# A long-convolution and expert-selection kernel: the filter layers in array quarters, earlier spectrum loads, and a shorter search round

## The chip, the cores and the metric

The kernel runs on one core of one Trainium2 chip. The metric is the device time of one execution, in microseconds (us). TensorE (PE) multiplies, VectorE (DVE) and ScalarE (ACT) can read the multiplier's result memory (PSUM), GpSimd (POOL) works on the on-chip buffer memory (SBUF) only, and SyncE (SP) issues nearly all transfers. Each engine takes its instructions in program order; between engines there are semaphores.

## The reference

```
h_mlp  = maximum(pos_emb @ w1, 0) @ w2          # 12608 x 64 -> 64 -> 128 channels
h_filt = h_mlp * exp(-0.01 * pos)[:, None]      # the decay
u = x * v                                       # 4 batches x 12608 x 128
y = irfft(rfft(u, 2S) * rfft(h_filt, 2S))[:S]   # causal convolution of every channel
a = x * y
scores = a @ w_gate                             # one number for each position
idx = the 128 positions of a batch with the largest scores
ye = maximum(a[idx] @ w1m, 0) @ w2m             # 128 -> 1024 -> 128
out = a;  out[idx] = a[idx] + sigmoid(scores[idx]) * ye
```

## The kernel before

The convolution's transform of length 25530 is split as 111 x 230, and every array lies as 111 x 115 positions. The program is written out in order by hand; the order of the code is the order on each engine.

1. **Filter layers** (`h_hid`). The positions come in 15 chunks of four columns of 111 positions in each of two halves h (the last chunk has two). Both halves share one input tile: half 0 on partitions 0 to 63, half 1 on 64 to 127. L282 multiplies a chunk by a block matrix with `w1` twice on its diagonal, 128 x 128, 444 columns; an ACT relu (L283) takes it to SBUF; then L291 multiplies by `w2`, eight matmuls of 64 rows, 128 columns. Before the second layer of chunk k-1 stands the first layer of chunk k. L300 and L304 (DVE) and L302 (POOL) multiply the result by the decay, with and without a sign pattern, and write it to `hb`: two DVE instructions for half 0, one for half 1, and from the latter one POOL instruction.
2. **Filter transform** (`h_spec`). For 32 groups of four channels: fold (L327, on DVE for groups 0 and 1, else on POOL), first transform (L336), ACT copy (L339), second transform (L356), then ACT L358 and four DVE instructions (L361 to L364), and the spectrum of the group goes to the DRAM tile `hd` (L365). The buffers of this result are the three named `ht`.
3. **Main loop**, 128 steps t (4 batches x 32 groups): transform the data (`f_s1`, L226/L227, and `dft`, L243), combine (L376, L377), multiply by the spectrum (`f_y`, L384 to L387; the spectrum is loaded from `hd` into `ht` by `load_h`, L221, two steps ahead), POOL L393/L394, back transform `f_i` (three steps later). `load_u` (L209) loads the data four steps ahead, `stage_u` (L215, L216, POOL) prepares them. Before the loop, L769 loads zeros (`zr`) into the padding rows of the `xa` buffers, which the next part uses.
4. **End of a batch** (`P1.run`), 29 steps h: last transform stage, L456 multiplies by x, L459 (DVE) by the gate weights, four ACT instructions (L473) sum each row into the scores; then L495 masks them.
5. **Search** (`TopK`, `TopKS`): 16 rounds find the 128th largest score bit pair by bit pair. A round counts scores over three candidates (L560), PE sums the counts over the partitions, L570 gives the step `up`, L577 (`move`) adds it to the next candidates. For batches 0 to 2 the rounds run on ACT in the background of the next batch (`TopKS`); for batch 3 they run alone on DVE at the end (`TopK`).
6. **Selection and experts** (`select`, `place`, `moe`): the positions are gathered (L711), transposed (L723), put through the two expert layers and scattered back. Batch 3's part has a run of 12 matmuls with no result that is used (L720, `NWARM`) ahead of the transposition.

Of the kernel before, what the change touches and what calls it, by code (L numbers as in the profile page):

```python
# [12 lines left out]
ALU = mybir.AluOpType  # L13
# [5 lines left out]
NQ = 64  # L19
# [24 lines left out]
NWARM = 12  # L44
# [91 lines left out]
def hyena_moe(ctx, tc, xg, x2, pos, bw, ww, wg, mw1, mw2, fo, c1, gx, cf, ci, wm, tk, zr, out):  # L136
# [112 lines left out]
    def h_hid():  # L249
        pt, hid = view(arena, POS0, [128, PJ, N1]), view(arena, HID0, [128, PJ, N1])  # L250
        wl = buf("u", NU - 1, [128, 2, 128])
        nc.gpsimd.memset(hb[:, :, :, N3:], 0.0)
        bwt, wwt = wl[:, 0], wl[:, 1]
        nc.sync.dma_start(bwt, bw)
        ch = [(a, min(a + PC, PJ)) for a in range(0, PJ, PC)]
# [22 lines left out]
        for k in range(len(ch) + 1):  # L278
            if k < len(ch):
                a, z = ch[k]  # L280
# [3 lines left out]
            if not k:  # L284
                continue
            a, z = ch[k - 1]
            ps = ps2(k % 2, [N1, 2, PC, D], f"hm_{k}")
            for i in range(z - a):
                for h in range(2):
                    if h * PJ + a + i < N3:  # L290
                        nc.tensor.matmul(ps[:, h, i], lhsT=hid[h * FO:(h + 1) * FO, a + i],  # L291
                                         rhs=wwt[h * FO:(h + 1) * FO], start=True, stop=True)
            for h in range(2):
                j0 = h * PJ + a
                j1 = min(h * PJ + z, N3)
                w = j1 - j0
                o = hb[:, :, :, j0:j1]
                pv = ps[:, h, :w].rearrange("p j d -> p d j")
                wb = wm_sb[:, :, j0:j1].unsqueeze(2).to_broadcast([N1, 3, D, w])
                nc.vector.tensor_tensor(out=o[:, 0], in0=pv, in1=wb[:, 0], op=ALU.mult)  # L300
                if h:
                    nc.gpsimd.tensor_tensor(out=o[:, 1], in0=o[:, 0], in1=wb[:, 1], op=ALU.mult)  # L302
                else:
                    nc.vector.tensor_tensor(out=o[:, 1], in0=pv, in1=wb[:, 2], op=ALU.mult)  # L304

    def h_spec():
# [39 lines left out]
        for g in range(NG):  # L346
# [13 lines left out]
            ht = buf("ht", g, [128, 2, HC])  # L360
# [5 lines left out]
            if g >= NG - 3:  # L366
                stage_u(g - NG + 3)

# [39 lines left out]
    class P1:  # L408
# [42 lines left out]
        def fin(self, h):  # L451
            ja, n = hbs[h]
            k = ja // 8
            xa = self.xa[k]
# [4 lines left out]
            nc.vector.tensor_tensor(out=wx, in0=xa[:, js], in1=self.wg.unsqueeze(1).to_broadcast([128, n, D]),  # L459
                                    op=ALU.mult)  # L460
            self.acc = wx, ja, n
            if ja + n == blocks[k][1]:
                j0, j1 = blocks[k]
                for t in range(2):
                    nc.sync.dma_start(out[self.b, t * PR:(t + 1) * PR, j0:j1], xa[t * NQ:t * NQ + PR, :j1 - j0])
                if k:
                    self.load_a(k - 1 + NX)
# [9 lines left out]
        def run(self, bg):  # L477
# [16 lines left out]
            self.reduce()  # L494
# [30 lines left out]
    class TopK:  # L525
# [32 lines left out]
        def counts(self, r):  # L558
            for i in range(3):
                nc.vector.tensor_scalar(out=self.ms[i % 2], in0=self.key, scalar1=self.cand[:, i + 1:i + 2], scalar2=0.0,  # L560
                                        op0=ALU.is_ge, op1=ALU.add, accum_out=self.cnt[:, i:i + 1])
            if r % 8 < 7:
                nc.vector.tensor_scalar(out=self.nx, in0=steps[:, r % 8 + 1], scalar1=self.cand[:, 0:1], scalar2=None,
                                        op0=ALU.add)
# [9 lines left out]
        def move(self, r):  # L574
            if r % 8 < 7:
                self.cand = self.cd[r % 2]
                nc.vector.tensor_scalar(out=self.cand, in0=self.nx, scalar1=self.up, scalar2=None, op0=ALU.add)  # L577
            else:
                nc.vector.tensor_tensor(out=self.top, in0=self.cand[:, 0:1], in1=self.up, op=ALU.add)
# [48 lines left out]

    def select(b, k, n, tr, ones, rs, ws):
# [17 lines left out]
        mm2(ps[:, 0:1], tr, cnt[:, 1:2], start=False, stop=True)  # L647
        lim = small([128, 1], f"lim_{b}", tag="lim")
# [17 lines left out]
        t = tots(sn[:, n - 1:n], tr, 1, f"bs_{b}", 3)[0][1]  # L666
        en = small([128, 1], f"en_{b}", tag="en")
# [37 lines left out]
    def moe(b, ix, ws, mb, ks):  # L705
# [11 lines left out]
        if b + 1 == B:  # L717
            wp = ps1(1, [128, 128], "warm")
            for _ in range(NWARM):
                nc.tensor.matmul(wp, lhsT=ident, rhs=ident, start=True, stop=True)  # L720
# [43 lines left out]
    for t in bank1 + bank2:  # L764
# [11 lines left out]
    for t in range(NT + LAG):  # L776
# [4 lines left out]
        if t < NT:  # L781
# [16 lines left out]
            load_h(t + 2)  # L798
# [24 lines left out]
def _layout(inputs):  # L823
# [14 lines left out]
    bw = np.zeros((2 * FO, 2 * FO), w1.dtype)  # L838
    bw[:FO, :FO] = w1
    bw[FO:, FO:] = w1  # L840
    named = [("xg", xg), ("x2", x2), ("pos", pg), ("bw", bw), ("ww", np.concatenate([w2, w2]))]
# [30 lines left out]
```

## Time and profile before

| | |
|---|---|
| three runs, median (lowest to highest) | 1013.59 us (1012.2 to 1017.33) |
| the profiled execution: its own time | 1017.58 us |
| its span, first to last instruction | 1015.6 us |
| TensorE's granted clock over the span | 0.97 of full |
| busy: PE, DVE, POOL, ACT | 932.6, 891.0, 745.7, 598.2 us |

Line numbers (L282) are those of the kernel before. In the rows below, a row of the timeline or of the chain begins with its start and its length in microseconds; xN is the number of instructions merged into it, and an fp32 matmul counts twice there; in brackets stands the idle time of the engine ahead of it, and what ended that. The granted clock is 1.00 at 2.4 GHz and 0.50 at 1.2 GHz.

### The profile page before, as it was taken

Reading aid. Unit: us, or ns where it says so; the run is one execution under the profiler, and the core shown is the slowest. Engines: PE = TensorE matmul, PEld = TensorE weight load, DVE = VectorE, ACT = ScalarE, POOL = GpSimd, SP = SyncE. Lnnn points to the kernel's source line nnn. Section 1 sums busy time; section 2 is a strip of 40 time slices with the busy share of each in tenths; the row PEclk is TensorE's granted clock in tenths of the full one; section 3 lists DMA queues with packets and bytes.
Section 4 is the critical chain, followed back from the end, with each engine's and each line's share of the span. In section 5 each row is a group of like instructions: output and inputs, shape, how many; then the busy total and the mean of one; then the engine's idle time right before and its main releaser. Section 6 shows DMA issues by size and latency. Waiting matters only on the chain.

```text
span 1015.6 us, 38023 instructions
## 1 busy us (share of the span) xinstructions
PE 932.6 (92%) x15620; PEld 823.2 (81%) x15620; DVE 891.0 (88%) x1563; ACT 598.2 (59%) x1961; POOL 745.7 (73%) x704
## 2 busy tenths in 40 slices
PE   8799979999999999999989999999999999989914
PEld 5577759988889898888889888888898888879804
DVE  7799969999998899999987999999878999986883
ACT  2255525555547887854478878544588786446710
POOL 4888838988887488988965689889765888754500
PEclk9899989999999999999999999999999999999956
DMA  8044486665776865657778656568686666544820
GB/s 240 2 168 177 183 220 179 194 181 176 217 217 222 282 179 173 196 167 199 222 234 266 194 179 196 171 183 242 198 280 197 190 181 183 162 150 140 292 69 6
DMA packets 64961, 190.58 MB, mean 188 GB/s; under 512 B 8725, under 2 KB 15876, under 8 KB 64772
## 3 DMA queue, kind: packets, MB, share of 16 engines
q1 hardware_dynamic: 64532, 187.63, 60.3%
q8 instruction: 123, 2.02, 0.9%
q0 software_dynamic: 256, 0.52, 0.2%
q14 instruction: 50, 0.41, 0.1%
HBM read 146.70 MB, written 41.42 MB: 185 GB/s over the span
## 4 chain that ended last, share of the span: by engine, by line
DVE 43%; PE 39%; DMA 10%; issue 4%; ACT 1%; SPq 1%; DVEq 1%; POOL 0%; POOLq 0%; ACTq 0%
DVE arena L384 8%; PE a L226 8%; DVE c L385 8%; PE a L243 7%; PE c L226 7%; DMA arena<-in_x_dram 6%; DVE c L377 5%; DVE c L376 5%; DVE arena L387 4%; DVE arena L386 4%; PE a L448 3%; DMA out_dram<-arena 3%; PE a L336 3%; PE c L336 3%; DVE arena L456 3%
## 5 line engine op out<-in xcount | busy, mean ns | idle before, releaser
L243 PE MATMUL a<-arena,cf_sb 128*64 128x222 f32 x2048 | 230.2, 356 | 19.1 <-DVE c L377 17.8
L226 PE MATMUL c<-ci_sb,arena 128*56 128x116 f32 x2048 | 226.3, 264 | 5.1 <-DVE arena L387 2.5
L227 PE MATMUL c<-ci_sb,arena 128*55 128x116 f32 x2048 | 226.3, 264 | 0.0
L393 POOL TENSOR_TENSOR arena<-arena 128x444 f32<-128x444 f32 x127 | 133.7, 1053 | 117.3 <-DVE st L617 56.1
L235 ACT COPY arena<-a 128x444 f32<-128x444 f32 x256 | 135.1, 530 | 143.2 <-PE a L227 140.6
L227 PE MATMUL a<-c_sb,arena 111*57 111x111 f32 x2048 | 218.5, 260 | 1.0 <-issue 1.0
L226 PE MATMUL a<-c_sb,arena 111*58 111x111 f32 x2048 | 218.7, 260 | 0.0
L226 PEld LDWEIGHTS c<-ci_sb,arena 128*56 128x56 f32 x2048 | 208.3, 131 | 6.3 <-ACT big L403 3.2
L226 PEld LDWEIGHTS a<-c_sb,arena 111*58 111x58 f32 x2048 | 200.6, 132 | 10.4 <-issue 0.3
L227 PEld LDWEIGHTS c<-ci_sb,arena 128*55 128x55 f32 x2048 | 208.2, 130 | 0.0
L227 PEld LDWEIGHTS a<-c_sb,arena 111*57 111x57 f32 x2048 | 200.5, 131 | 1.5 <-issue 1.2
L243 PEld LDWEIGHTS a<-arena,cf_sb 128*64 128x64 f32 x2048 | 134.4, 137 | 75.7 <-DVE c L377 46.5
L403 ACT COPY big<-c 128x928 f32<-128x928 f32 x128 | 118.3, 924 | 76.7 <-PE c L227 74.6
L448 PE MATMUL a<-big,gx_sb 128*64 128x128 f32 x2496 | 157.1, 273 | 5.7 <-DVE arena L456 4.2
L473 ACT ACTIVATE arena<-arena 128x128 f32<-128x128 f32 x464 | 137.8, 298 | 40.3 <-DVE arena L459 33.1
L215 POOL TENSOR_TENSOR arena<-arena 111x460 f32<-111x460 f32 x128 | 150.0, 1172 | 2.2 <-DMA arena<-in_xg_dram 2.1
L448 PEld LDWEIGHTS a<-big,gx_sb 128*64 128x64 f32 x2496 | 142.7, 137 | 8.7 <-DVE arena L456 6.1
L384 DVE TENSOR_TENSOR arena<-c,arena 128x888 f32<-128x888 f32 x128 | 138.5, 1082 | 11.6 <-DMA arena<-hd 7.2
L216 POOL TENSOR_TENSOR arena<-arena,wm_sb 111x460 f32<-111x460 f32 x128 | 139.2, 1088 | 10.1
L385 DVE TENSOR_TENSOR c<-c,arena 128x888 f32<-128x888 f32 x128 | 138.3, 1080 | 0.0
L431 POOL TENSOR_TENSOR arena<-big 128x384 f32<-128x384 f32 (+1 forms) x104 | 99.9, 985 | 51.3 <-PE a L443 49.9
L394 POOL TENSOR_TENSOR arena<-arena 128x444 f32<-128x444 f32 x127 | 133.7, 1053 | 0.0
(135 smaller groups left out, 1531.1 us busy)
## 6 DMA issues: line engine op xcount, KB each, us to landing
arena<-hd SPq DMA_DIRECT2D x128, 444.0 KB
arena<-in_xg_dram SPq DMA_DIRECT2D x128, 402.5 KB
arena<-in_x_dram SPq DMA_DIRECT2D x112, 224.0 KB
out_dram<-arena SPq DMA_DIRECT2D x112, 224.0 KB
hd<-arena SPq DMA_DIRECT2D x32, 444.0 KB
arena<-in_moe_w_dram SPq DMA_DIRECT2D x8, 512.0 KB
arena<-in_pos_dram SPq DMA_DIRECT2D x14, 222.0 KB
arena<-in_x_dram SPq DMA_DIRECT2D x8, 112.0 KB
```

The costliest lines, as they stand in the source:

```text
L215: nc.gpsimd.tensor_tensor(out=u[:, 0], in0=u[:, 0], in1=u[:, 1], op=ALU.mult)
L216: nc.gpsimd.tensor_tensor(out=u[:, 1].rearrange("p (s j) -> p s j", s=4), in0=u[:, 0].rearrange("p (s j) -> p s j", s=4), in1=sg, op=ALU.mult)
L226: nc.tensor.matmul(o[:h], lhsT=lhsT[:, :h], rhs=rhs, **kw)
L227: nc.tensor.matmul(o[NQ:NQ + m - h], lhsT=lhsT[:, h:], rhs=rhs, **kw)
L235: nc.scalar.copy(out=te[:, e], in_=tps[e])
L243: nc.tensor.matmul(pq[w][e * NQ:(e + 1) * NQ, c], lhsT=cf_sb[:, 2 * w + e], rhs=te[:, e, c], start=True, stop=True)
L384: nc.vector.tensor_tensor(out=mt, in0=uv, in1=ht[:, 0].unsqueeze(1).to_broadcast([128, 2, HC]), op=ALU.mult)
L385: nc.vector.tensor_tensor(out=uv, in0=uv, in1=ht[:, 1].unsqueeze(1).to_broadcast([128, 2, HC]), op=ALU.mult)
L393: eng.tensor_tensor(out=nat(sd[:, 0]), in0=nat(yz[:, 0]), in1=rev(yz[:, 1]), op=ALU.add)
L394: eng.tensor_tensor(out=nat(sd[:, 1]), in0=rev(yz[:, 0]), in1=nat(yz[:, 1]), op=ALU.subtract)
L448: nc.tensor.matmul(ps[t * NQ:(t + 1) * NQ, k], lhsT=gx_sb[:, o:o + NQ], rhs=ay[:, :, e * NJ + j], start=e == 0, stop=e == 1)
L473: nc.scalar.activation(out=wx[:, k], in_=wx[:, k], func=AF.Copy, accum_out=self.sc[:, ja + k:ja + k + 1])
```

## The change

- **First filter layer.** `w1` comes once per half (64 columns), and a pair of chunks is multiplied at a time: four matmuls of 64 rows by 64 columns, one in each quarter of the array. In the second chunk of a pair the halves lie swapped in `hid`, and L291's counterpart picks them accordingly. The short chunk is now the first.
- **Decay.** For half 1, four ACT instructions (a copy with the decay as a scale for each partition, 128 columns) take the place of a DVE instruction; in the last chunk a DVE instruction takes the place of POOL's.
- **Matmuls without a used result**: 24 (bf16) ahead of the first layer, 12 after the last chunk, 3 and 2 in batch 3's `select`; L720's run has 8 in place of 12.
- **Spectra.** The filter transform writes from the `sd` buffers. Its last three steps also issue `load_h` for steps 0 to 2, and `zr` is loaded in step 8 of the main loop.
- **Scores.** For the last step h of a batch the gate product and its sum are four DVE instructions (scalar_tensor_tensor with an accumulator) in place of L459 and four of ACT.
- **Search of batch 3.** `move` is gone from 14 of 16 rounds: the comparison is (key - up) >= candidate, one scalar_tensor_tensor.

```diff
@@ h_hid @@
...
-        ch = [(a, min(a + PC, PJ)) for a in range(0, PJ, PC)]
+        ch = [(max(a, 0), a + PC) for a in range(PJ % PC - PC, PJ, PC)]
...
-                hp = ps1(k % 2, [128, PC * N1], f"hid_{k}")[:, :(z - a) * N1]
-                nc.tensor.matmul(hp, lhsT=bwt, rhs=pt[:, a:z].rearrange("p j i -> p (j i)"), start=True, stop=True)
-                nc.scalar.activation(out=hid[:, a:z].rearrange("p j i -> p (j i)"), in_=hp, func=AF.Relu)
+        def first(p):
+            cs = ch[2 * p:2 * p + 2]
+            hp = [ps1(p % 2 * 2 + i, [128, PC * N1], f"hid_{p}_{i}")[:, :(z - a) * N1] for i, (a, z) in enumerate(cs)]
+            for h in range(2):
+                r = slice(h * FO, (h + 1) * FO)
+                for i, (a, z) in enumerate(cs):
+                    nc.tensor.matmul(hp[i][(h ^ i) * FO:((h ^ i) + 1) * FO], lhsT=bwt[r],
+                                     rhs=pt[r, a:z].rearrange("p j i -> p (j i)"), start=True, stop=True)
+            for i, (a, z) in enumerate(cs):
+                nc.scalar.activation(out=hid[:, a:z].rearrange("p j i -> p (j i)"), in_=hp[i], func=AF.Relu)
+        def warm(n, w):
+            wp = ps1(3, [w.shape[0], w.shape[1]], "warm")
+            for _ in range(n):
+                nc.tensor.matmul(wp[:w.shape[1]], lhsT=w, rhs=w, start=True, stop=True)
+        warm(24, onesb)
+        first(0)
+        for k, (a, z) in enumerate(ch):
...
+            if end:
+                warm(12, c1_sb)
...
-                nc.vector.tensor_tensor(out=o[:, 0], in0=pv, in1=wb[:, 0], op=ALU.mult)
                 if h:
-                    nc.gpsimd.tensor_tensor(out=o[:, 1], in0=o[:, 0], in1=wb[:, 1], op=ALU.mult)
+                    for i in range(w):
+                        nc.scalar.activation(out=o[:, 0, :, i], in_=ps[:, 1, i], func=AF.Copy,
+                                             scale=wm_sb[:, 0, j0 + i:j0 + i + 1])
+                    if end:
+                        nc.vector.tensor_tensor(out=o[:, 1], in0=pv, in1=wb[:, 2], op=ALU.mult)
+                    else:
+                        nc.gpsimd.tensor_tensor(out=o[:, 1], in0=o[:, 0], in1=wb[:, 1], op=ALU.mult)
                 else:
-                    nc.vector.tensor_tensor(out=o[:, 1], in0=pv, in1=wb[:, 2], op=ALU.mult)
+                    for e in range(2):
+                        nc.vector.tensor_tensor(out=o[:, e], in0=pv, in1=wb[:, 2 * e], op=ALU.mult)
+            if k % 2 == 0 and k // 2 + 1 < (len(ch) + 1) // 2:
+                first(k // 2 + 1)
@@ h_spec @@
-            ht = buf("ht", g, [128, 2, HC])
+            ht = buf("sd", g, [128, 2, HC])
...
             if g >= NG - 3:
                 stage_u(g - NG + 3)
+                load_h(g - NG + 3)
@@ P1.fin @@
+            if h == len(hbs) - 1:
+                for k in range(n):
+                    nc.vector.scalar_tensor_tensor(out=wx[:, k], in0=xa[:, ja % 8 + k], scalar=1.0, in1=self.wg, op0=ALU.mult,
+                                                   op1=ALU.mult, accum_out=self.sc[:, ja + k:ja + k + 1])
@@ TopK.counts @@
+                if r % 8:
+                    nc.vector.scalar_tensor_tensor(scalar=self.up, in1=self.cand[:, i + 1:i + 2].to_broadcast([128, self.n]),
+                                                   op0=ALU.subtract, op1=ALU.is_ge, **kw)
             if r % 8 < 7:
+                c, nx = self.cand[:, 0:1], self.cd[r % 2]
+                if r % 8:
+                    nc.vector.scalar_tensor_tensor(out=nx, in0=steps[:, r % 8 + 1], scalar=self.up,
+                                                   in1=c.to_broadcast([128, 4]), op0=ALU.add, op1=ALU.add)
@@ TopK.move @@
-            if r % 8 < 7:
-                self.cand = self.cd[r % 2]
-                nc.vector.tensor_scalar(out=self.cand, in0=self.nx, scalar1=self.up, scalar2=None, op0=ALU.add)
@@ main loop @@
-    for r in (PR, NQ + PR):
-        nc.sync.dma_start(arena[r:r + NQ - PR, OFF["xa"][0]:OFF["xa"][0] + NX * 8 * D], zr)
-    load_h(0)
-    load_h(1)
...
-            load_h(t + 2)
+            if t:
+                load_h(t + 2)
+            if t == 8:
+                for r in (PR, NQ + PR):
+                    nc.sync.dma_start(arena[r:r + NQ - PR, OFF["xa"][0]:OFF["xa"][0] + NX * 8 * D], zr)
```

In the middle of the filter layers, TensorE's instructions are these before (L282 is the first layer of a chunk, L291 the second; the names are PSUM banks):

```order
L282 MATMUL a_70<-arena 128x444
L291 MATMUL c_74<-arena 111x128 x8
L282 MATMUL a_71<-arena 128x444
L291 MATMUL c_75<-arena 111x128 x8
L282 MATMUL a_70<-arena 128x444
```

and these now (L285 is the first layer, L303 the second):

```order
L285 MATMUL a_70<-arena 64x444
L285 MATMUL a_71<-arena 64x444
L285 MATMUL a_70<-arena 64x444
L285 MATMUL a_71<-arena 64x444
L303 MATMUL c_75<-arena 111x128 x8
L303 MATMUL c_74<-arena 111x128 x8
L285 MATMUL a_72<-arena 64x444
```

The first layer of two chunks now stands together, ahead of two second layers, and alternates between two pairs of banks. ScalarE does one relu (L283) for each chunk before; now its queue reads (L288 is the relu, L314 the decay):

```order
L288 ACTIVATE arena<-a_70 128x444
L288 ACTIVATE arena<-a_71 128x444
L314 ACTIVATE big<-c_75,wm_sb 111x128 x4
L314 ACTIVATE big<-c_74,wm_sb 111x128 x4
L288 ACTIVATE arena<-a_72 128x444
```

Eight decay instructions have come between the relus of one pair and those of the next. SyncE's queue at the passage from the filter transform to the main loop, before (`hd` is the spectrum, L209 the data):

```order
L365 DMA hd<-arena 128x888 x32
L769 DMA arena<-in_zr_dram 8x4096 x2
L221 DMA arena<-hd 128x888 x2
L209 DMA arena<-in_xg_dram 112x920
L221 DMA arena<-hd 128x888
```

and now:

```order
L385 DMA hd<-arena 128x888 x30
L221 DMA arena<-hd 128x888
L385 DMA hd<-arena 128x888
L221 DMA arena<-hd 128x888
L385 DMA hd<-arena 128x888
L221 DMA arena<-hd 128x888
L209 DMA arena<-in_xg_dram 112x920 x2
```

The first spectrum loads have moved ahead of the last two stores, and the two loads of zeros have gone from here.

## Rows read from the trace of the kernel before

**Rows 1.** The page, part 1: busy time, share of the span, instructions.

```profile
PE 932.6 (92%) x15620; PEld 823.2 (81%) x15620; DVE 891.0 (88%) x1563; ACT 598.2 (59%) x1961; POOL 745.7 (73%) x704
```

**Rows 2.** The chain that ended last, filter layers: start, length, what.

```profile
3.99 3.30 PE a L282 x4
...
21.67 0.94 PE a L282 x2
22.62 1.06 PE c L291 x16
```

**Rows 3.** Timeline, the same stretch: DVE and POOL.

```profile
20.92 1.49 DVE L300 TENSOR_TENSOR big<-c,wm_sb 111x512 f32<-111x512 f32 x2
...
23.69 1.49 POOL L302 TENSOR_TENSOR big<-big,wm_sb 111x512 f32<-111x512 f32 x1 [0.49 <-DVE big L300]
```

**Rows 4.** Timeline, from the filter layers' end into the filter transform.

```profile
35.77 0.66 PE L291 MATMUL c<-arena 64*111 64x128 f32 x6 [0.45 <-DVE big L300]
...
39.44 5.17 DVE L327 TENSOR_TENSOR arena<-big 111x464 f32<-111x464 f32 x4 [1.02 <-POOL big L302]
...
47.72 0.98 PE L356 MATMUL a<-arena 58*64 58x222 f32 x16
```

**Rows 5.** Windows: stretch, length, busy by engine, granted clock, DMA share, GB/s.

```profile
41.20:47.20 6.00, 5.56 (x60) 5.40 (x61) 3.41 (x3) 1.06 (x2) 6.00 (x5) 0.50 0.00 0
```

**Rows 6.** The chain, filter transform, one group.

```profile
52.94 0.91 PE a L356 x16
53.86 1.67 PE a L336 x32
```

**Rows 7.** Timeline of ACT: two copies, and an instruction with a per-partition operand.

```profile
47.82 0.96 ACT L339 COPY arena<-c 128x444 f32<-128x444 f32 x2 [2.41 <-PE c L336]
...
354.16 0.29 ACT L614 ACTIVATE st<-tk_sb 128x4 f32<-128x4 f32 x1
354.35 0.92 ACT L403 COPY big<-c 128x928 f32<-128x928 f32 x1
```

**Rows 8.** Timeline of SP and DVE at the start of the main loop.

```profile
132.10 0.90 SPq L769 DMA_DIRECT2D arena<-in_zr_dram  x2
133.11 1.99 SPq L221 DMA_DIRECT2D arena<-hd  x2
...
140.35 1.08 DVE L384 TENSOR_TENSOR arena<-c,arena 128x888 f32<-128x888 f32 x1 [7.20 <-DMA arena<-hd]
...
147.17 0.32 SPq L221 DMA_DIRECT2D arena<-hd  x1
...
159.36 1.08 DVE L384 TENSOR_TENSOR arena<-c,arena 128x888 f32<-128x888 f32 x1
```

**Rows 9.** Windows, behind the loads of zeros.

```profile
133.00:139.00 6.00, 5.45 (x60) 3.62 (x57) 0.15 (x1) 2.34 (x6) 0.00 (x0) 1.00 0.97 150
```

**Rows 10.** Timeline of DVE, end of batch 0.

```profile
349.04 0.69 DVE L459 TENSOR_TENSOR arena<-arena,c 128x512 f32<-128x512 f32 x1
351.07 0.28 DVE L495 TENSOR_TENSOR sc<-sc,tk_sb 128x116 f32<-128x116 f32 x1 [1.34 <-ACT arena L473]
```

**Rows 11.** Timeline of DVE, search of batch 3, and a count on fp32.

```profile
972.55 0.23 DVE L577 TENSOR_SCALAR st<-st 128x4 f32<-128x4 f32 x1
972.82 0.33 DVE L560 TENSOR_SCALAR_CACHE_REDUCE ms<-hi,st 128x116 bf16<-128x116 int16 x1
...
973.08 0.33 DVE L560 TENSOR_SCALAR_CACHE_REDUCE ms<-hi,st 128x116 bf16<-128x116 int16 x1
...
996.51 0.34 DVE L639 TENSOR_SCALAR_CACHE_REDUCE arena<-c,st 128x116 f32<-128x116 f32 x1
```

**Rows 12.** Timeline of DVE: a scalar_tensor_tensor with an accumulator.

```profile
1005.28 0.29 DVE L729 SCALAR_TENSOR_TENSOR arena<-arena,wgb 128x128 f32<-128x128 f32 x1 [2.87 <-DMA arena<-out_dram,ix]
```

**Rows 13.** Timeline of PE ahead of the last batch's experts.

```profile
1001.57 5.38 PE L720 MATMUL a<-ident 128*128 128x128 f32 x24
...
1006.79 0.27 PE L723 MATMUL a<-ident,arena 128*128 128x128 f32 x1
```

More of the change, by code (lines that the diff above doesn't have):

```diff
@@ L290, in h_hid @@
                     if h * PJ + a + i < N3:
[L291 to L296, printed above, removed]
+                        r = slice((h ^ k % 2) * FO, ((h ^ k % 2) + 1) * FO)
+                        nc.tensor.matmul(ps[:, h, i], lhsT=hid[r, a + i], rhs=wwt[r], start=True, stop=True)
+            end = k + 1 == len(ch)
+            if end:
+                warm(12, c1_sb)
+            w = min(PJ + z, N3) - PJ - a
+            for h, j0, j1 in ((0, a, z), (1, PJ + a, PJ + a + w)):
                 o = hb[:, :, :, j0:j1]
-                pv = ps[:, h, :w].rearrange("p j d -> p d j")
-                wb = wm_sb[:, :, j0:j1].unsqueeze(2).to_broadcast([N1, 3, D, w])
-                nc.vector.tensor_tensor(out=o[:, 0], in0=pv, in1=wb[:, 0], op=ALU.mult)
+                pv = ps[:, h, :j1 - j0].rearrange("p j d -> p d j")
+                wb = wm_sb[:, :, j0:j1].unsqueeze(2).to_broadcast([N1, 3, D, j1 - j0])
                 if h:
-                    nc.gpsimd.tensor_tensor(out=o[:, 1], in0=o[:, 0], in1=wb[:, 1], op=ALU.mult)
-                else:
-                    nc.vector.tensor_tensor(out=o[:, 1], in0=pv, in1=wb[:, 2], op=ALU.mult)
+                    for i in range(w):
[5 more added lines that the diff above has]
+                        nc.gpsimd.tensor_tensor(out=o[:, 1], in0=o[:, 0], in1=wb[:, 1], op=ALU.mult)
+                else:
+                    for e in range(2):
+                        nc.vector.tensor_tensor(out=o[:, e], in0=pv, in1=wb[:, 2 * e], op=ALU.mult)
+            if k % 2 == 0 and k // 2 + 1 < (len(ch) + 1) // 2:
+                first(k // 2 + 1)
     def h_spec():
@@ L574, in move @@
         def move(self, r):
-            if r % 8 < 7:
-                self.cand = self.cd[r % 2]
-                nc.vector.tensor_scalar(out=self.cand, in0=self.nx, scalar1=self.up, scalar2=None, op0=ALU.add)
-            else:
-                nc.vector.tensor_tensor(out=self.top, in0=self.cand[:, 0:1], in1=self.up, op=ALU.add)
+            if r % 8 == 7:
+                nc.vector.tensor_tensor(out=self.top, in0=self.nx[:, 0:1], in1=self.up, op=ALU.add)
         def rounds(self):
@@ L627, in move, with warm @@
                 nc.scalar.activation(out=self.top, in_=self.ge[:, 0:1], func=AF.Copy, scale=-1.0, bias=0.5)
+    def warm(n):
+        wp = ps1(1, [128, 128], "warm")
+        for _ in range(n):
+            nc.tensor.matmul(wp, lhsT=ident, rhs=ident, start=True, stop=True)
     def select(b, k, n, tr, ones, rs, ws):
@@ L666, in select @@
         t = tots(sn[:, n - 1:n], tr, 1, f"bs_{b}", 3)[0][1]
+        if b + 1 == B:
+            warm(2)
         en = small([128, 1], f"en_{b}", tag="en")
@@ L717, in moe @@
         if b + 1 == B:
-            wp = ps1(1, [128, 128], "warm")
-            for _ in range(NWARM):
-                nc.tensor.matmul(wp, lhsT=ident, rhs=ident, start=True, stop=True)
+            warm(NWARM)
         yield "p"
@@ L762, in topk_one @@
         yield from moe(b, ix, ws, mb, (3, (3, 3, 1, 2)[b]))
-    for t in bank1 + bank2:
+    for t in bank1[3:] + bank1[:3] + bank2:
         nc.vector.memset(t, 0.0)
```

52 lines of the change are left out of this document (25 added, 27 removed).

## The prediction

> **What bounds the kernel now.** I read the page's busy shares first: TensorE (PE) 92%, VectorE (DVE) 88%, neither at its end [rows 1]. A mean over stages hides what bounds each, so I went on to the chain that ended last, the timelines of the stretches that the diff touches, and windows for the clock. The reader is to see four things.
>
> The filter layers run at the pace of PE: 0.94 us for a chunk's first layer and 1.06 us for its second stand end to end on the chain, 2.00 us a chunk [rows 2]. Beside that, POOL is busy for 1.49 us of each chunk and waits 0.49 us, and a DVE instruction takes 0.75 us and less, three to a chunk [rows 3]: DVE is nearly full too, so that relieving PE alone would bring little. At the end of this stage the second layer's last matmuls start at 35.77, and the fold only at 39.44, behind POOL; the second transform of group 0 follows at 47.72 [rows 4]. In between PE stands nearly idle, and then works at a granted clock of 0.50, half speed, from 41.2 to 47.2 [rows 5].
>
> At the start of the main loop DVE waits 7.20 us for the first spectrum, whose load was issued at 133.11, behind two loads of zeros [rows 8].
>
> At a batch's end DVE waits 1.34 us for ACT's four row sums, four times in all [rows 10].
>
> In the search of batch 3 only DVE and, for a moment, PE work: every instruction there is on the path [rows 11].
>
> **The change part by part.** The sum is made against the profiled execution, 1017.58 us, and taken over to the runs at the end.
>
> *Filter layers, pace.* The first layer in quarters is new. The nearest row is the second transform (L356), whose matmuls also use four quarters: 16 matmul records of 222 columns take 0.91 us [rows 6]. A pair of chunks now has 8 records of 444 columns, the same number of columns, so 0.91 us for two chunks where it was 2 x 0.94. A pair costs PE 0.91 + 2 x 1.06 = 3.03 us. DVE falls to two instructions, some 1.3 us a chunk. POOL keeps 1.49. ScalarE gets eight decay instructions and two relus a pair. Two copies of 444 columns take 0.96 us, so a relu costs 0.47 [rows 7]. For the decay the nearest row is an ACT instruction with an operand for each partition: four columns of it hold the engine for 354.35 - 354.16 = 0.19 us [rows 7], and 124 columns more cost between (0.92 - 0.29) / 924 = 0.7 and 0.92 / 928 = 1.0 ns each by the long copy there: 0.27 to 0.31 us, I take 0.29. ACT needs 8 x 0.29 + 2 x 0.47 = 3.26 us a pair and becomes the bound, by a little: 1.63 us a chunk. Its waits for the first two chunks, which can't yet overlap, I put at 1.5 us.
>
> That decay price is uncertain, as no row has a scale operand for each partition, only a bias. The Trainium skill (ScalarE: Activation LUTs, What ACT_TABLE_LOAD costs) says that each such pointer operand, scale or bias, adds about 93 ns to an instruction. By it a decay copy costs what I took; without it, 0.2 us, ACT would need 2.5 us a pair and PE's 3.03 would bind, 1.7 us less in all.
>
> *Filter layers, start.* Before, PE starts at 3.99 when the input lands and takes 3.30 us for four records, which is half speed (two take 0.94 later) [rows 2]. The 24 added matmuls have no row of their kind; L720's fp32 ones take 5.38 / 24 = 0.22 us a record at half speed [rows 13], and a bf16 one should cost between a half and all of that. So they end between 4.4 and 7 us; I take the first, since it needs one pass where fp32 shows two records. The first pair then runs from 4.4 at half speed to 6.2. ACT has from there 57 decay copies, 14 relus at 0.47 and one short one at 0.3: 16.5 + 6.9 us, with the 1.5 of waits 31.1. PE's last second layer ends two ACT bunches of copies before (1.16 + 0.87, plus its own length 0.9), at 30.0. Behind it DVE has 2 x 0.6 and 0.55 us, where before DVE and POOL needed from 36.4 to 39.44: the fold starts at 31.9 in place of 39.44. **-7.5 us.** Ends: 9 if PE binds and everything fits, 4.5 if the start is late (7 us) and ACT's copies cost 0.33.
>
> *Into the transform.* The 12 added matmuls keep PE at work for some 2.5 us behind the layers (24 records of 111 columns; the transform's 32, if two run side by side, take 1.67, so 0.1 each [rows 6]). From the fold's start to L356 it was 47.72 - 39.44 = 8.28 us, with the clock at 0.50 [rows 4, 5]. At full speed DVE's four folds (5.17 us) set the end, and one transform of 1.67 us follows [rows 4, 6]: 6.85. **-1.4 us**, and nothing if the clock falls all the same.
>
> *Spectra.* The load for step 0 now goes out two stores earlier, some 6 us, and without the zeros ahead of it. These are slow: behind them the DMA engines are 0.97 busy but move only 150 GB/s [rows 9]. The needed moment does not move, so nearly the whole wait goes: **-7.1 us** (6 to 7.2). What is late next is DVE itself: L384 comes 159.36 - 140.35 = 19.0 us later for the fourth time, 4.75 us a step, which is what its six instructions need. In step 8 the zeros stand ahead of step 9's loads. A spectrum load issued at 147.17 serves the L384 at 159.36 [rows 8], 12.2 us of cover for some 6 us of zeros: I cost this at nothing, and at up to 2 us if the data's load, which has less cover, is caught.
>
> *Scores.* From L459's start to L495 it was 2.03 us [rows 10]. Now four scalar_tensor_tensor with accumulator stand there; the nearest row has 0.29 us for 128 columns [rows 12]. 4 x 0.29 and the accumulator's reading come to 1.25. ACT's sums of the step before end under them. **-0.8 us, four times: -3.2** (2.4 to 4.2). DVE sets the pace behind it in the loop, and the search behind it at the end, so it should stay.
>
> *Search.* `move` holds DVE for 972.82 - 972.55 = 0.27 us [rows 11] in 14 rounds: 3.8 us. A count starts 0.26 us behind the one before [rows 11]; as scalar_tensor_tensor it should take 0.29 where it took 0.33 [rows 11, 12], so 42 x 0.04 = 1.7 us. The next candidates are computed while PE sums. **-5.5 us** (3.8 to 6.1).
>
> A rule speaks against that form. The Trainium skill (VectorE: DVE Perf Modes, The perf-mode tier table) allows tensor_scalar up to four times the pace on 16-bit data in SBUF, and an operation with two tensors less. The rows show nothing of such a pace: the count on int16 takes 0.33 us, that on fp32 0.34 [rows 11].
>
> *Ahead of the experts.* L720's 12 matmuls end about when the transposition starts, 1006.79, though the gathered rows were there at 1005.28 [rows 12, 13]. Eight end at 1001.57 + 8 x 0.45 = 1005.15. That is 1.5 us, less if the clock then rises later than it did; the 3 and 2 matmuls in `select` lie under DVE's scans. **-1.3 us** (0.5 to 1.8).
>
> **Sum**: 7.5 + 1.4 + 7.1 + 3.2 + 5.5 + 1.3 = 26.0 us. The profiled execution would go from 1017.6 to 991.6. It lies 4.0 us over the median of the three runs, 1013.59; the same saving from there gives **987.5 us**.
>
> **The rivals.**
>
> *The filter layers gain half.* The quarters overlap only two at a time, or ACT waits for PE and PE for ACT in turn. At 1.86 us for the pair's first layer a chunk takes 2.0 us again on PE, and only the shorter end (1.9 against 3.0) and the start are left, 2 us of 7.5. For it: the alternation of banks and row halves is in another order than L356's. Against it: L356 overlaps four. Result 993.
>
> *The loads collide.* The first spectrum still comes late behind three stores, or the zeros in step 8 stop the loop: 4 to 7 us given back, 992 to 994. Against it: the 12.2 us of cover.
>
> *The new DVE form is slow.* If the counts were helped by their form and lose it, by 0.1 us each, 42 of them give back 4.2 us and the 1.7 are not won: 993.4. For it speaks only that no row has this form on int16 and a broadcast operand.
>
> *The decay on ACT makes it slower.* ACT writes single elements 464 bytes apart, where DVE wrote runs of four; no row of ACT has that. The other terms give 18.5 us, and the shorter end of the layers some 1. The kernel is slower than before from the point where a chunk on ACT costs 2.0 + 19.5 / 14.5 = 3.3 us, so a copy 0.72 us in place of 0.29; at 1 us it would be 1013.6 - 19.5 + 14.5 x 2.5 = 1030. Against it: ACT's 1.63 us a chunk has only the stride as an unknown.
>
> **How the numbers follow.** Forecast 68%, with a range of its own of 982 to 993; half the gain in the layers 12%; colliding loads 9%; the slow form 7%; slower through ACT 4%. The best ends add to 30 us, which from the lowest run is 982; the poor ends (4.5, 0, 5, 2.4, 3.8, 0.5) to 16, which gives 997. The range is 981 to 997. Half a per cent, 5 us, is about what a measurement here can tell from no change; all but the last rival lie well beyond it. Two mishaps together could reach the middle: faster 0.93, same 0.03, slower 0.04.
>
> **What would show it.** Right: the fold starts near 32 us; ACT is nearly full in the layers, with eight decay copies of some 0.37 us at 0.29 spacing; the granted clock stays at 1.00 to the first transform; L384's counterpart waits under 1 us at the start of the loop; the mask of the scores comes 1.25 us behind the first of the four new instructions; a search round is shorter by 0.39 us; the transposition starts within 0.2 us of the gather's landing. Wrong: a pair of chunks over 3.6 us; a clock of 0.50 behind the fold; a DMA wait in steps 8 to 12; a count longer than 0.33 us.

## The result: less than half of the forecast saving, and the profile after

The changed kernel takes 1002.71 us (median of 6 runs, 1000.52 to 1007.54), the kernel before 1014.13 (6 runs): a ratio of 0.9889, 95% interval [0.9857, 0.9921], or 11 us less where 26 were forecast. The profiled execution took 1006.59 us, 11.0 less than that of before. It is the right sign, outside the range.

The page's first part, which answers to [rows 1], tells little: DVE has 10 us less to do, ACT 11 more.

```profile
PE 932.2 (93%) x15700; PEld 824.5 (82%) x15700; DVE 880.8 (88%) x1565; ACT 609.4 (61%) x1986; POOL 743.2 (74%) x703
```

**The filter layers.** The chain of the changed kernel, against [rows 2] (start, length, what):

```profile
24.02 1.32 ACT big L314 x4
25.34 0.38 ACT arena L288
25.76 1.16 PE c L303 x16
26.94 1.30 DVE big L322 x2
28.32 1.33 ACT big L314 x4
29.65 0.38 ACT arena L288
30.07 1.15 PE c L303 x16
```

Three engines follow each other where two should stand side by side. From one L288 to the next a pair of chunks takes 4.31 us; before it took two times 2.00. The timeline says who waits for whom, against [rows 3]:

```profile
26.02 1.32 ACT L314 ACTIVATE big<-c,wm_sb 111x128 f32<-111x128 f32 x4
26.94 1.29 DVE L322 TENSOR_TENSOR big<-c,wm_sb 111x512 f32<-111x512 f32 x2 [1.01 <-PE c L303]
28.32 1.33 ACT L314 ACTIVATE big<-c,wm_sb 111x128 f32<-111x128 f32 x4 [0.97 <-DVE big L322]
```

The ACT copies of a chunk wait for DVE's two products of the same chunk, though they take the other half of it from PSUM and write other columns. Nothing that is computed asks for this.

**From there to the filter transform**, against [rows 4]; then two windows, against [rows 5]:

```profile
42.39 0.56 DVE L317 TENSOR_TENSOR big<-c,wm_sb 111x384 f32<-111x384 f32 x1 [1.18 <-ACT big L314]
43.05 5.17 DVE L347 TENSOR_TENSOR arena<-big 111x464 f32<-111x464 f32 x4
...
51.42 1.76 PE L376 MATMUL a<-arena 58*64 58x222 f32 x16
```

```profile
44.00:46.00 2.00, 0.89 (x18) 0.75 (x18) 2.00 (x2) 0.00 (x0) 2.00 (x2) 1.00 0.00 0
...
49.00:51.00 2.00, 2.00 (x25) 2.00 (x22) 0.00 (x0) 0.00 (x0) 2.00 (x3) 0.50 0.00 0
```

The fold starts 3.6 us later than before. The granted clock is now full when the fold starts, but falls at 46.4, within it. The second transform comes 8.4 us behind the fold's start, as before (8.3), and itself runs at half speed (1.76 us against 0.98).

**Start of the main loop**, against [rows 8]:

```profile
131.60 0.37 SPq L221 DMA_DIRECT2D arena<-hd  x1
...
136.55 0.37 SPq L221 DMA_DIRECT2D arena<-hd  x1
```

```profile
135.49 0.61 DVE L384 TENSOR_TENSOR arena<-c,arena 128x444 f32<-128x444 f32 x1
...
137.71 1.08 DVE L405 TENSOR_TENSOR arena<-c,arena 128x888 f32<-128x888 f32 x1
```

The first f_y (L405, L384 before) waits for no load and starts 2.6 us earlier than before, although the filter transform ends 4.5 us later.

**Scores and search** of batch 3, against [rows 10, 11]:

```profile
960.95 0.29 DVE L482 SCALAR_TENSOR_TENSOR arena<-arena,c 128x128 f32<-128x128 f32 x1
...
961.98 0.28 DVE L520 TENSOR_TENSOR sc<-sc,tk_sb 128x116 f32<-128x116 f32 x1
...
964.27 0.16 DVE L607 SCALAR_TENSOR_TENSOR st<-a,tk_sb 128x3 f32<-128x3 f32 x1 [0.16 <-PE a L227]
...
964.47 0.34 DVE L587 SCALAR_TENSOR_TENSOR ms<-hi,st 128x116 bf16<-128x116 int16 x1
...
964.74 0.33 DVE L587 SCALAR_TENSOR_TENSOR ms<-hi,st 128x116 bf16<-128x116 int16 x1
...
965.65 0.16 DVE L607 SCALAR_TENSOR_TENSOR st<-a,tk_sb 128x3 f32<-128x3 f32 x1 [0.17 <-PE a L227]
...
986.61 0.34 DVE L678 TENSOR_SCALAR_CACHE_REDUCE arena<-c,st 128x116 f32<-128x116 f32 x1
```

From the first L482 to the mask it is 1.03 us, where it was 2.03. A round (L607 to L607) takes 1.38 us, where it was 1.63; a count takes what it took, 0.34 us at a spacing of 0.26 to 0.27.

**Ahead of the experts**, against [rows 12, 13]: the transposition starts 0.11 us behind the gathered rows.

```profile
991.67 3.78 PE L666 MATMUL a<-ident 128*128 128x128 f32 x16
...
995.33 0.29 DVE L770 SCALAR_TENSOR_TENSOR arena<-arena,wgb 128x128 f32<-128x128 f32 x1 [2.82 <-DMA arena<-out_dram,ix]
...
995.44 0.30 PE L764 MATMUL a<-ident,arena 128*128 128x128 f32 x1
```

So the 11 us divide as follows; each line is the difference of two starts (after less before), less that of the line above.

| from the line above to | starts, before and after | forecast | measured |
|---|---|---|---|
| fold | 39.44, 43.05 | -7.5 | +3.6 |
| second transform of group 0 | 47.72, 51.42 | -1.4 | +0.1 |
| last product of the filter transform (L364, L384) | 131.0, 135.5 | 0 | +0.8 |
| first f_y | 140.35, 137.71 | -7.1 | -7.1 |
| mask of batch 3 | 968.43, 961.98 | -3.2 | -3.8 |
| first count behind the search | 996.51, 986.61 | -5.5 | -3.5 |
| transposition | 1006.79, 995.44 | -1.3 | -1.5 |
| sum | | -26.0 | -11.4 |

### The profile page after: what moved, and what is told of

It is laid out like the page before. It is cut to its first block, busy times and chain, and to the rows that moved or that the text cites. A ratio compares the mean times of both kernels' runs of the same rounds, so it can differ in the third digit from the quotient of the medians.

```text
span 1004.3 us, 38259 instructions
## 1 busy us (share of the span) xinstructions
PE 932.2 (93%) x15700; PEld 824.5 (82%) x15700; DVE 880.8 (88%) x1565; ACT 609.4 (61%) x1986; POOL 743.2 (74%) x703
## 3 DMA queue, kind: packets, MB, share of 16 engines
q8 instruction: 124, 2.03, 0.9%
## 4 chain that ended last, share of the span: by engine, by line
PE 45%; DVE 39%; DMA 8%; issue 3%; ACT 2%; POOL 1%; SPq 1%; DVEq 0%; POOLq 0%; ACTq 0%
PE a L226 10%; PE a L243 9%; PE c L226 8%; DVE arena L405 7%; DVE c L406 7%; PE a L469 5%; DVE c L398 5%; DVE c L397 5%; DVE arena L408 4%; DMA arena<-in_x_dram 4%; DVE arena L407 4%; PE c L356 3%; PE a L356 2%; DMA out_dram<-arena 2%; DVE arena L477 2%
## 5 line engine op out<-in xcount | busy, mean ns | idle before, releaser
L499 ACT ACTIVATE arena<-arena 128x128 f32<-128x128 f32 x448 | 133.0, 298 | 40.0 <-DVE arena L485 32.6
L469 PEld LDWEIGHTS a<-big,gx_sb 128*64 128x64 f32 x2496 | 142.3, 137 | 11.4 <-DVE arena L477 9.1
L405 DVE TENSOR_TENSOR arena<-c,arena 128x888 f32<-128x888 f32 x128 | 138.5, 1082 | 4.4
```

The costliest lines, as they stand in the source:

```text
L405: nc.vector.tensor_tensor(out=mt, in0=uv, in1=ht[:, 0].unsqueeze(1).to_broadcast([128, 2, HC]), op=ALU.mult)
L469: nc.tensor.matmul(ps[t * NQ:(t + 1) * NQ, k], lhsT=gx_sb[:, o:o + NQ], rhs=ay[:, :, e * NJ + j], start=e == 0, stop=e == 1)
L499: nc.scalar.activation(out=wx[:, k], in_=wx[:, k], func=AF.Copy, accum_out=self.sc[:, ja + k:ja + k + 1])
```

## The experiments

Ratios are to the kernel before, measured beside each; 0.001 is 1 us. The difference of two ratios is uncertain by some 4 us, their two intervals taken together (5 with e2), so where a smaller difference is told, the rows of the profile carry it. Lines of code are those of the changed kernel.

**e1: own PSUM tiles for the two halves.**

```diff
-                hp = [ps1(p % 2 * 2 + i, ...)[:, :(z - a) * N1] ...]
+                hp = [ps2(p % 2, [128, 2, 512], ...)[:, i, :(z - a) * N1] ...]
-            ps = ps2(k % 2, [N1, 2, PC, D], f"hm_{k}")
+            ps = [ps1(k % 2 * 2 + h, [N1, PC, D], f"hm_{k}_{h}") for h in range(2)]
```

> The changed kernel, with the two halves of a chunk's second product in two PSUM tiles of one bank each (before: two halves of one tile of two banks), and the first product's pair in the tile that comes free. Nothing of the computation changes. Theory A: in the changed kernel ScalarE's four copies wait for VectorE's two products of the same chunk because both read one PSUM tile, and the program orders the readers of a tile on two engines; that puts 1.15 + 1.30 + 1.33 + 0.38 us and the hand-overs in a row, 4.31 us for a pair of chunks. With own tiles the copies run beside the products: the pair is then bounded by ScalarE, 8 x 0.32 + 2 x 0.4 = 3.4 us, the folds start 7 x 0.9 = 6.4 us earlier (about 36.7 us) and the kernel takes 5 to 7 us less than the changed one (about 996.5). Rival B: the order comes from the interleaved columns that both engines write in the same rows; then the wait stays, the pair stays at 4.3 and the time at 1002.7. Rival C: the pair is bounded by the quarters of the array or by the loads; then the pair stays over 4 us although the copies no longer wait for VectorE.

993.52 us, ratio 0.9759 [0.9736, 0.9783]. The chain of the layers:

```profile
20.47 0.91 PE c L285 x8
21.38 2.17 PE a L303 x32
23.55 0.91 PE c L285 x8
24.45 2.17 PE a L303 x32
```

Its timeline there, and behind the layers:

```profile
22.47 2.48 DVE L322 TENSOR_TENSOR big<-a,wm_sb 111x512 f32<-111x512 f32 x4 [0.59 <-PE a L303]
22.65 2.42 ACT L314 ACTIVATE big<-a,wm_sb 111x128 f32<-111x128 f32 x8
...
34.73 5.17 DVE L347 TENSOR_TENSOR arena<-big 111x464 f32<-111x464 f32 x4
...
41.62 0.98 PE L376 MATMUL a<-arena 58*64 58x222 f32 x16
```

ACT and DVE now work at the same time, a pair takes 3.07 us, bounded by PE with ACT just as full, and the fold starts 8.3 us earlier than in the changed kernel. The two engines still write interleaved columns: rival B falls. What ordered them was the PSUM tile that both read. It was not a need of the reads: the halves were 512 columns apart in that tile, and in e1 each has a tile of 512 columns to itself. The program's own order (no times are in it) shows the same for the first copy of a chunk: the changed kernel's waits for DVE and PE, that of e1 for PE alone.

```text
changed:  L314 ACTIVATE big<-c_74,wm_sb 111x128 [waits DVE_49,PE_49]
e1:       L314 ACTIVATE big<-a_71,wm_sb 111x128 [waits PE_49]
```

Rival C falls too: the pair was not held by the quarters or the loads.

**e11, e12: the changed kernel and e1 again, on one chip.**

> The changed kernel once more, beside e9 and e12 on the same chip, so that they can be compared with it directly. Every theory: its ratio to the kernel before is 0.986 to 0.992 as before, its folds start at 43 to 44 us, and from there to the second transform of the first group it takes 6.9 or 8.3 us, as the granted clock falls or not.

> The kernel of e1 once more, beside the changed kernel on the same chip. Theory: own PSUM tiles take the first fold from 43 to 44 us to 34.7 us and the second transform with it; ratio 0.974 to 0.979, 10 to 13 us less than the changed kernel's run of the same call. If e1's ratio owed something to its place among the runs, the difference comes out under 8 us.

e11: 1005.20 us, 0.9895 [0.9861, 0.9929]; e12: 993.69 us, 0.9793 [0.9764, 0.9822]. The medians differ by 11.5 us, the fold's start by 9.2. First e11, then e12:

```profile
43.60 5.18 DVE L347 TENSOR_TENSOR arena<-big 111x464 f32<-111x464 f32 x4
...
50.49 0.98 PE L376 MATMUL a<-arena 58*64 58x222 f32 x16
```

```profile
34.36 5.17 DVE L347 TENSOR_TENSOR arena<-big 111x464 f32<-111x464 f32 x4
```

In e11, with the same instructions as the changed kernel, the clock held and the second transform came 6.9 us behind the fold.

**e2: the second half's decay back on VectorE, shared tile kept.**

```diff
-                    for i in range(w):
-                        nc.scalar.activation(out=o[:, 0, :, i], in_=ps[:, 1, i], func=AF.Copy, scale=...)
+                    nc.vector.tensor_tensor(out=o[:, 0], in0=pv, in1=wb[:, 0], op=ALU.mult)
```

> The changed kernel with the decay of a chunk's second half back on VectorE (one product of 111 x 512 in place of four copies on ScalarE); the quarters of the array and the shared tile stay. Theory A: VectorE is then the bound with three products of 0.65 us a chunk, 1.95 us, 3.9 to 4.0 us a pair against 4.31: the folds start 2 to 3 us earlier (40.0 to 41.0 us) and the time falls by 2 to 3 us, to about 1000; that is, ScalarE's share as it was made costs more than it saves. Rival C: if the quarters or the loads bound the stage, the pair stays at 4.3 us and the time at 1002.7.

998.10 us, ratio 0.9823 [0.9781, 0.9865]; the fold starts at 38.6. DVE alone stands on the chain, 1.80 us a chunk (a product of three starts 0.60 behind the one before, not 0.65):

```profile
23.25 0.60 DVE big L313
23.85 1.20 DVE big L320 x2
25.05 0.60 DVE big L313
25.64 1.20 DVE big L320 x2
```

So with a shared tile ACT's share costs 4.4 us at the fold (43.05 against 38.6) over leaving the work on DVE, and with own tiles it saves 3.9 (34.73 in e1 against 38.6).

**e6: own tiles, first product whole.** The first product is one matmul with 128 x 128 weights a chunk, as before the change.

```diff
-                    nc.tensor.matmul(hp[i][(h ^ i) * FO:((h ^ i) + 1) * FO], lhsT=bwt[r], rhs=pt[r, a:z]...)
+                nc.tensor.matmul(hp[i], lhsT=bwt, rhs=pt[:, a:z]...)
```

> The kernel of e1 (own PSUM tiles) with the first product of the layers as before the change: one matmul of 128 x 128 weights a chunk in place of two of 64 x 64 that run side by side with the other chunk's two. Nothing of the computation changes. Theory: with the copies free, TensorE bounds the pair, and the quarters are what makes it 0.97 us for two chunks: without them the pair takes 2 x 0.94 + 2 x 1.13 = 4.1 us in place of 3.07, the folds start about 7 us later (41 to 42 us), and the ratio rises from 0.976 to about 0.983. Rival: ScalarE's eight copies and two activations (3.07 us in a row) bound the pair and the quarters give nothing; then the pair stays under 3.4 us and the folds start before 37 us.

996.01 us, ratio 0.9826 [0.9790, 0.9861]; a pair takes 1.69 + 1.93 = 3.62 us on PE, the fold starts at 37.9. The quarters are worth 0.55 us a pair, 3.2 us in all and half of what was expected, since whole products are cheaper than that: the first product's four records take 1.69 us, not 2 x 0.94, and the second product's 32 take 1.93 us when they stand together, not 2 x 1.13.

**e7: another order of the loads at the start** (own tiles; the decay table from ScalarE's queue, three later tables behind the positions).

```diff
+    nc.scalar.dma_start(wm_sb, wm)
     gp = cp.tile([128, 1], F32, name="gp")
...
-        nc.sync.dma_start(wm_sb, wm)
```

> The kernel of e1 with the decay table sent from ScalarE's queue ahead of its table load, and the three tables of the later stages (48, 64 and 128 KB) sent behind the last chunk of positions instead of ahead of the sixth. Theory: what is left between the forecast's 31.9 us for the first fold and the 34.73 us of e1 is the start, where chunks two to five wait for their positions (landed at 8.80, 9.33 and 14.4 us); sending less ahead of them gives 0.8 to 2 us: the folds start at 32.7 to 33.9 us. Rival: the start is slow because TensorE's products take twice their steady time there (16 of L303 in 2.0 us against 1.13), whatever is loaded; then the folds start at 34.4 to 34.9 us.

995.69 us, ratio 0.9818 [0.9796, 0.9841]: the fold starts at 36.0, later than either theory had it. The decay table, now ahead in the stream, delayed the first positions:

```profile
6.45 2.22 PE L285 MATMUL c<-arena 64*64 64x222 f32 x8 [2.04 <-DMA arena<-in_pos_dram]
...
10.26 1.76 PE L285 MATMUL c<-arena 64*64 64x444 f32 x8
11.94 3.75 PE L303 MATMUL a<-arena 64*111 64x128 f32 x32
```

The second pair's products (10.26) wait for no load any more and still take nearly twice their steady time (0.97 us in e1), which speaks for the rival as far as it goes.

**e9: the gaps of the start filled** (own tiles).

```diff
         first(0)
+        warm(4, onesb, bank1[3])
...
+            if k == 0:
+                warm(8, onesb, bank1[3])
```

> The kernel of e1 with matmuls of ones that nothing reads in the two places where TensorE stands idle at the start: four behind the first pair's first product, eight behind the first chunk's second product. Theory: what e1 still lacks against the forecast's first fold (34.73 against 31.9 us) is that TensorE's products run at half their steady pace until about 13 us (16 of L303 in 2.0 us against 1.13), since the 24 matmuls at the start do not bring the clock up and the gaps behind them let it start over; with the gaps filled the steady pace comes earlier: the folds start 1 to 2.5 us earlier, at 32.2 to 33.7 us. Rival: filling the gaps changes nothing, since the pace comes up when it does whatever stands in the gaps, or the added matmuls delay the products behind them: then the folds start at 34.5 to 35.3 us.

The steady pace is there at 10.7 us, and the fold starts at 33.1 (L285 and L304 are the first and the second product):

```profile
4.34 1.03 PE L285 MATMUL c<-arena 64*64 64x222 f32 x8
...
6.47 0.62 PE L293 MATMUL a<-onesb 128*128 128x128 bf16 x8
9.21 1.51 PE L285 MATMUL c<-arena 64*64 64x444 f32 x8 [2.13 <-DMA arena<-in_pos_dram]
10.66 2.00 PE L304 MATMUL a<-arena 64*111 64x128 f32 x32
```

The same first product in e1:

```profile
4.33 1.93 PE L285 MATMUL c<-arena 64*64 64x222 f32 x8
```

Half of the 2.8 us that e1 lacks against the forecast's fold is this pace (the fold starts 1.6 us earlier than in e1, 1.2 earlier than in e12). That the added matmuls brought it is not shown: the first product stands ahead of them, has the same instructions ahead of it in both kernels, and was already fast in e9. In e2, which has nothing added in the gap, the product behind the gap was fast too (1.59 us at 9.43, against 2.28 in e1), and the granted clock fell to 0.50 only at 11.2. What is left of the 2.8 us stands beside the wait for the second pair's positions, 2.13 us above; no run brought them earlier. The time did not follow: 993.79 us, 0.9782 [0.9751, 0.9813], against e12's 993.69. In the profile 1.2 us are there at the end of the filter transform (last product at 123.3, e12 124.5) and gone by the first mask (337.4, e12 337.7). Between the first f_y and that mask the twelve profiles with the new scores scatter by 2.4 us (209.6 to 212.0), twice what there is to find.

**e3: the search as before.** `counts` and `move` are those of the kernel before.

```diff
-                    nc.vector.scalar_tensor_tensor(out=nx, ..., scalar=self.up, in1=c.to_broadcast([128, 4]), ...)
+                nc.vector.tensor_scalar(out=self.cand, in0=self.nx, scalar1=self.up, scalar2=None, op0=ALU.add)
```

> The changed kernel with the search as before: the step added to the candidates in an instruction of its own after each total, and the counts as comparisons with one scalar. If the whole of the 3.46 us by which the search got shorter is the 14 additions that left the chain (0.25 us each), the time rises by 3.3 to 3.6 us, to about 1006.2, a round goes from 1.385 back to 1.63 us, and the counts take the same 0.33 us as 0.34. If the counts of the new form had gained something by themselves (my forecast put 1.7 us there), it rises by over 5 us. If the difference stood in something else (the place of the search, the clock), it stays within 1 us.

1009.14 us, ratio 0.9926 [0.9909, 0.9942], 3.8 us over the changed kernel's 0.9889. A round is back at 1.63 us and a count takes 0.33. By the rows, 14 rounds of 0.25 us, the whole gain is the addition that left the chain.

**e4: the scores as before.** `fin` has one product for all heads again, and `run` calls `reduce` behind it.

> The changed kernel with the last block's scores as before: one product and one sum, and not four instructions that do both. Theory: the four take 1.03 us from the first to the mask where the old way took 2.03, so each of the four batches gets 0.9 to 1.0 us longer, 3.6 to 4.0 us in all, to about 1006.5. Rival: batch 0 gained nothing in the changed kernel (its first y and its mask were both 2.6 us early), so the gain of the form is smaller than its own rows show where VectorE waits for something else at that place; then three batches at most lose 1 us, 3 us or less.

1010.64 us, ratio 0.9938 [0.9919, 0.9957], 5 us over the changed kernel, uncertain by 4. From the last product to the mask it is 2.03 us again:

```profile
964.05 0.69 DVE L480 TENSOR_TENSOR arena<-arena,c 128x512 f32<-128x512 f32 x1
966.08 0.28 DVE L516 TENSOR_TENSOR sc<-sc,tk_sb 128x116 f32<-128x116 f32 x1 [1.34 <-ACT arena L494]
```

The mask waits for ACT in all four batches, so the form gains its 1.0 us at each of them. Whether batch 0 as a whole gets shorter, which the rival doubts, is open: from the first f_y to its mask it takes 212.4 us here, 210.7 in the kernel before and 209.6 to 212.0 in the twelve profiles with the new form (all but these two). The other three batches show more than the rows of the form: from the mask of batch 0 to that of batch 3 it is 617.4 us here and in the kernel before, and 610.0 to 613.5 in the twelve. What gains the rest is open.

**e5: the spectra loaded late, the zeros still in step 8.**

```diff
-                load_h(g - NG + 3)
...
+    load_h(0)
+    load_h(1)
```

> The changed kernel with the first three spectra loaded where the kernel before loads them, after the whole filter transform, and the rest kept (the zeros still go out in step 8). Theory: the early loads are worth the whole of the wait that they remove, 7.1 us by the rows of the forecast, and nothing pays for it elsewhere: the wait of the first f_y for its spectrum comes back and the ratio to the kernel before goes from 0.989 to 0.996. Rival: with the zeros' two slow transfers out of the way the late loads wait only for the last store, so that a part of the 7.1 us belongs to the zeros' new place: then 3 to 5 us come back, ratio 0.992 to 0.994.

1006.32 us, ratio 0.9917 [0.9890, 0.9944], 2.8 us over the changed kernel, which alone would not be clear of the uncertainty. The wait that comes back is 2.97 us, not 7.1: the rival.

```profile
140.45 1.08 DVE L404 TENSOR_TENSOR arena<-c,arena 128x888 f32<-128x888 f32 x1 [2.97 <-DMA arena<-hd]
```

**e10: the zeros back behind the filter transform, the spectra early.**

> The changed kernel with the zeros' two transfers back where the kernel before has them, behind the filter transform and ahead of the first steps, and the first three spectra still loaded early. Theory: the first f_y waited because its spectrum stood behind the zeros in the queue (4.2 us of the 7.2) and behind the last store (3.0 us, the wait that e5 shows); each part is removed by itself, and a spectrum that is loaded early is not touched by the zeros: the time stays within 1 us of the changed kernel and no wait of f_y comes back. Rival: the zeros delay the first loads of u and the later spectra behind them, and up to 4.2 us come back at the second to fourth step.

1004.64 us, ratio 0.9910 [0.9884, 0.9936], beside e11's 1005.20: no difference that can be told. The first f_y starts without a wait:

```profile
136.10 1.08 DVE L405 TENSOR_TENSOR arena<-c,arena 128x888 f32<-128x888 f32 x1
```

Of the 7.2 us that DVE waited before, 4.2 were the zeros ahead of the load and 3.0 the load's late issue; loading early removes both, and the zeros' new place adds nothing to it that shows.

**e8: TensorE kept busy in the last search** (own tiles).

```diff
             self.tot = tots(self.cnt, self.ones, 3, f"tot_{self.b}", 3)[0][1]
+            if self.b + 1 == B and r >= 8:
+                warm(3)
```

> The kernel of e1 with three matmuls of 128 x 128 that nothing reads behind the total of each of the last eight rounds of the last search, where TensorE is otherwise idle for 1.0 of 1.39 us. Theory: the granted clock is 0.50 all through the last search, and in e1 it stays there until 986.6, 3.5 us into the experts; with TensorE busy it rises before the experts, whose first 17 pairs of products then take 0.11 us each in place of 0.21 (1.7 us), and the products of the last selection take some tenths less: 1.5 to 3 us less than e1. Rival: the three matmuls sit ahead of the next total and lengthen the rounds; then the search gets longer by up to 8 x 0.3 us and nothing is gained.

997.11 us, ratio 0.9832 [0.9808, 0.9856]: slower than e1 and e12, by the rival's way. Three such matmuls stand as six records of 1.65 us together, and the next total waits behind them; a round goes from 1.38 to 1.73 us. Nor did the clock follow the work: PE is busy for 17.7 of the 18 us from 966 on (six windows of 3 us, of which the first and the last stand here, with the 2 us behind them), and the granted clock (the column ahead of the last two) is still 0.50 at 984. It rises at 985.7, 0.8 us ahead of the experts' first product. So it does in e12, the kernel of e1 without these matmuls: at 982.0, 1.3 us ahead. The late rise that e8 was to mend, at 986.8 and 3.6 us into the experts, is that of e1's one profile and not of its code.

```profile
966.00:969.00 3.00, 3.00 (x14) 2.54 (x13) 2.17 (x16) 0.00 (x0) 0.00 (x0) 0.50 0.00 0
...
981.00:984.00 3.00, 2.97 (x15) 2.40 (x15) 0.97 (x5) 0.00 (x0) 0.84 (x1) 0.50 0.00 0
984.00:986.00 2.00, 1.99 (x10) 1.67 (x9) 0.28 (x2) 0.00 (x0) 0.13 (x1) 0.58 0.11 33
```

## Why the prediction was wrong

*Filter layers, pace: the step that failed.* "ACT needs 8 x 0.29 + 2 x 0.47 = 3.26 us a pair and becomes the bound": the sum took each engine's work by itself and let the three run beside each other. The prices were good. A decay copy lasts 0.51 us, but the next starts 0.27 us behind it; the quarters give 0.91 us for two chunks, as forecast; and with own tiles, e1, a pair takes 3.07 us. What was missing is the order of the readers of one PSUM tile. It puts PE, DVE and ACT in a row for every second chunk, 4.31 us a pair. The forecast asked how long ACT's copies take and not what they wait for, which the order of the program shows without any time. e1 and e12 price this step: 8.3 and 9.2 us of the 11.1 by which the fold was missed. The rival "the layers gain half" stood in the right place with another cause and far too small a loss.

*Filter layers, start: too small.* The forecast let the first pair run from 4.4 to 6.2 us, as it does (4.33 to 6.26 in e1), and gave all waits 1.5 us. In e1 the second pair's positions land at 8.80 us and PE's products take twice their steady time until some 13 us: 34.73 against 31.9. e12's profile has a granted clock of 0.50 from 10 to 12 us there; e1's reads 1.00 with products as slow, so that the lengths of the products, and not that column, are the sign. In e9 the steady pace came earlier, and with it the fold by 1.2 to 1.6 us.

*Into the transform: right where the clock holds.* The forecast had 6.85 us from the fold to the second transform. In nine profiles (e1, e3, e4, e6, e7, e8, e9, e11, e12) the granted clock stays at 1.00 and it is 6.9. In four it falls to 0.50 within the fold: in the changed kernel's own, e2 and e5 it stays down and it is 8.3 to 8.4, in e10 it is back at 49.0, early enough for 6.9. The code alone does not decide it, as e11 and the changed kernel are the same. All four are among the seven profiles with the shared tile, none among the six with own tiles; that is too few to say that the tile matters here too.

*Spectra*: right, as e5 and e10 show part by part. *Scores*: right in the rows (1.0 us at each mask, 0.8 forecast); the loop's further gain was not forecast and is not explained (e4). *Ahead of the experts*: right.

*Search: mis-sized.* The move's 14 x 0.25 us were right; the 1.7 us for faster counts were not there. The price was taken from a form with 128 columns of fp32 (0.29 us), and on 116 columns of int16 with a broadcast operand it is 0.34, what the old form took. The Trainium skill (VectorE: DVE Perf Modes, The perf-mode tier table) would let the old form run up to four times as fast on 16-bit data; no run here shows that, 0.33 us in e3 against 0.34.

Of the four signs of being wrong that were on record, three came: a pair over 3.6 us (4.31), a clock of 0.50 behind the fold, and a count longer than 0.33 us (0.34, barely). The fourth did not: in steps 8 to 12 DVE waits for no load. The range's lower end was rounded down: the best ends add to 29.7 us, which from the lowest run is 982.5, not 981.

With the one missing step repaired the time is 993.5 us (e1), within the range on record and 6 us over the forecast; 2 us for the search and 2.8 for the start are known parts of that.

## What to carry to other kernels

Two engines that take two halves of one PSUM tile may be run one after the other by the program, whatever they write; before adding a second engine to a stage, look at what its instructions wait for in the order of the built program, and give each reader its own tile. A sum of busy times is a forecast only for engines that nothing puts in a row. e1 is the version to keep: 0.9759 and 0.9793, measured twice, against 0.9889 and 0.9895 for the change as made.

## What the runs showed of the hardware

The granted clock stayed at 0.50 through 18 us in which PE was busy for 17.7 (e8, 966 to 984); in the changed kernel it rose at 995.3, after added matmuls at 987.6, 989.8 and 991.7. The same instructions behind the fold kept the full clock in one execution (e11) and lost it in another (the changed kernel's), which is worth 1.5 us there, 8.4 against 6.9. At the end e1 and e12 have the same instructions too, and from the transposition to the last instruction they take 10.7 us (clock up at 986.8, 4.4 us behind the transposition's start) and 8.9 us (clock up at 982.0, 0.6 us ahead of it). Neither was explained, and one profile of a kernel can mislead by that much.
